# Gathering the first expert's rows before the last two attention steps, and adding theirs by one-hot products

## The chip, the core and the metric

The kernel runs on one core of one Trainium2 chip. The time is device microseconds of one launch, as the median of several runs. The core has five engines that run side by side, each with its own instruction queue: TensorE (PE, matmuls, with its weight loads shown as PEld), VectorE (DVE), ScalarE (ACT), GpSimd (POOL) and SyncE (SP, which here issues DMAs only). ACT and POOL issue DMAs too; the ones with an index list ("indirect") are POOL's. An engine works through its queue in order, so an instruction that waits holds up all that stand behind it.

## The reference, cut to what is computed

Two blocks follow one another. The first is a recurrent attention cell over 4 batches, 8 heads, 768 steps and a head size of 40. The second takes its output as 3072 rows of 320 numbers, sends every row to one of 8 experts by a hash of its token id, and runs that expert's two layers.

```python
for t in range(S):                                   # S = 768, state C and n per batch and head
    m_new = np.maximum(f_gate[:, :, t] + m, i_gate[:, :, t])
    f_stab = np.exp(f_gate[:, :, t] + m - m_new)
    i_stab = np.exp(i_gate[:, :, t] - m_new)
    C = f_stab * C + i_stab * outer(v[t], k[t])
    n = f_stab * n + i_stab * k[t]
    y[:, :, t] = sigmoid(o_gate[t]) * (C @ q[t]) / max(abs(n . q[t]), 1)
x = y.transpose(0, 2, 1, 3).reshape(3072, 320)
expert_idx = token_ids * 2654435761 % 8
for e in range(8):
    mask = expert_idx == e
    out[mask] = np.maximum(x[mask] @ w1[e], 0) @ w2[e]   # w1: 320 x 1024, w2: 1024 x 320
```

## The kernel before

**Attention.** Each batch is cut into 6 chunks of 128 steps, so there are 24 loop steps `s` (batch `b = s // 6`, chunk `c = s % 6`). Within a chunk the recurrence is a masked product with decay weights; between chunks a small state `C` is carried. A loop step writes its instructions in a fixed order, by hand (`tc.manual_schedule()`): loads, `decayed`, the turns of keys and queries (`turn_k`, `turn_q`), the turn back and finish of rows of an earlier step (`back`, `finish`), `decays` and `state` and `entering` for the chunks ahead, the stores of the finished rows (SP's queue), `scores` and `weigh` of the next chunk (`weigh` is L379 on DVE), routing work hung on the step (the lists `before` and `after`), and last `attend`, the products of the step itself (L422 with the carried state, L429 with the weights) and their copy out of PSUM (`hT` or `hB`, L445). In steps 5, 11, 15 and 18, which also carry a sigmoid of an output gate on ACT, that copy and two others are DVE's.

**Turn back and finish.** `back` turns a block of heads x time into time x heads with four transposes (L454). `finish` forms the denominator (L460, L463), multiplies by the gate (L466), takes the reciprocal (L469) and multiplies (L471, on POOL, for the very last block on DVE), and its result `x` is stored to the DRAM tensor `x_rows` (L477). Rows of batch `b - 1` are finished during batch `b`, one block of 128 for each step. For the last batch each block is finished one step after its attention, so steps 19 to 23 finish two blocks and one is left after the loop. PSUM tiles of the turns, decays and finishes share four buffers (the tag "tr").

**Routing.** Beside the loop the kernel counts the rows of each expert and gives every row a slot: each expert has 3 x 128 main slots and 32 remainder slots (416 in all, `CAP`); the remainders of four experts share one block of 128. Steps 12 to 19 turn slots into one-hot tables (`route_hot`), whose products of steps 13 to 20 (`route_table`) give the table of the row for each slot. After step 20 `route_index` makes the gather indices `g_idx` and the scatter indices `s_idx` of it on DVE (L643 to L647).

**Experts.** `fetch` gathers an expert's rows from `x_rows` with indirect DMAs on POOL (L842): three blocks of 128 and, for experts 0 and 4, the shared remainder block `xr`. `turns` transposes each block on PE (L865, L868), with DVE first copying the last 64 of the 320 columns a second time (L867), since that half block is used from both halves of the partitions, and DVE or ACT copying the result to `xT` (L870, L872). Expert 0's first layer is `layer1`, with products over 416 columns (L884, L891); the others use `layer1_pairs`, a form with fewer products, on sums of weight blocks and sums of row blocks (`sums_of_w1` on POOL, L936; `sums_of_x` on DVE, L942 to L946). The second layer is `layer2_pair` for all, with sums of `w2` on POOL (L1028), products L1044 and L1054, and DVE ops on their results (L1071 to L1082). Rows are scattered to the output by indirect DMAs on POOL (L852). Turns, sums and weight loads of later experts are called at set places between products (`between`).

At the start of this part stands an order that the change touches:

```python
fetch(0)
fetch(1)
later = weight_slices(1) + weight_slices(2)
...
spin(11)
for piece in turns(0):
    piece()
    spin(1)
```

`spin` runs products (L1138) whose result nobody reads, into a PSUM bank of their own. The weights in `later` are issued from ACT's queue, three slices at a `between`; those of experts 3 and on are issued from SP's queue.

The gate steps at the kernel's start (`gates_a`, `gates_b`, `gates_x`) use tiles `f_sb`, `i_sb`, `m_sb`, `fP` and so on, which lie in a pool that ends with the attention part.

Of the kernel before, what the change touches and what calls it, by code (L numbers as in the profile page):

```python
# [8 lines left out]
F32 = mybir.dt.float32  # L9
# [13 lines left out]
def kernel(  # L23
# [55 lines left out]

    x_d = nc.dram_tensor("x_rows", (N, Dm), F32, kind="Internal").ap()  # L80

    ident = consts.tile([P, P], F32, name="ident")
    g_idx = consts.tile([P, NC], I32, name="g_idx")
    s_idx = consts.tile([P, NC], I32, name="s_idx")
    xe = consts.tile([1, NX + 1], I32, name="xe")

    def weights(src1, src2, wpool, w2pool):
# [29 lines left out]
    with tc.tile_pool(name="gates", bufs=1) as gp, \  # L117
# [19 lines left out]
        Rs = [gp.tile([P, 2, H, P], BF16, name=f"R{i}") for i in range(2)]  # L137
        f_sb = gp.tile([BH, S], F32, name="f_sb")
        i_sb = gp.tile([BH, S], F32, name="i_sb")
        m_sb = gp.tile([BH, S + 1], F32, name="m_sb")  # L140

        at = [0, 2 * BH, 3 * BH]
        fP, iP, aP, AP, r1, r3 = (
            gp.tile([P, W2], F32, name=name) for name in ("fP", "iP", "aP", "AP", "r1", "r3")
        )
        mP = gp.tile([P, W2 + 1], F32, name="mP")
        keep = gp.tile([P, W2], F32, name="keep")
        zA = gp.tile([P, 6, W2], BF16, name="zA")
# [261 lines left out]
        def attend(s):  # L410
# [25 lines left out]
            b = s // NB  # L436
            if b == LB:
                hT[b, c] = wk.tile([P, 2, 2, P], F32, name="hT")[:]
                to = hT[b, c]
            else:  # L440
                if c == 0:
                    hB[b] = wk.tile([P, 2, 2, S], F32, name="hB")
                hT[b, c] = hB[b][:, :, :, c::NB]
                to = hB[b][:, :, :, c * P : (c + 1) * P]
            from_psum(s)(to, d["ht"][:, :, : 2 * P].rearrange("p f (i t) -> p f i t", t=P))  # L445
# [11 lines left out]
        def finish(b, r, xo):  # L457
            hs = xo.rearrange("p f i (x d) -> p f (i x) d", d=DP)
            den = wk.tile([P, 2, PR, 1], F32, name="den")
            nc.vector.tensor_scalar(  # L460
                den[:], hs[:, :, :, D:D1], scalar1=-1.0, scalar2=1.0, op0=ALU.mult, op1=ALU.max,
            )
            nc.vector.tensor_tensor(den[:], den[:], hs[:, :, :, D:D1], op=ALU.max)  # L463
            x = wk.tile([P, H, D], F32, name="x")
            xv = x.rearrange("p (j f) d -> p f j d", f=2)
            nc.vector.tensor_tensor(  # L466
                xv, hs[:, :, :, :D], gate(b, r).rearrange("p (j f) d -> p f j d", f=2), op=ALU.mult,
            )
            nc.vector.reciprocal(den[:], den[:])  # L469
            eng = nc.vector if (b, r) == (LB, NB - 1) else nc.gpsimd  # L470
            eng.tensor_tensor(xv, xv, den[:].to_broadcast([P, 2, PR, D]), op=ALU.mult)  # L471
            rows = x_d[b * S : (b + 1) * S, :]
            if b == LB:
                rows = rows[r * P : (r + 1) * P, :]
            else:
                rows = rows.rearrange("(p r) d -> p r d", r=NB)[:, r, :]
            return lambda: nc.sync.dma_start(rows, x.rearrange("p h d -> p (h d)"))  # L477

# [161 lines left out]
        def route_index():  # L640

            ta = gp.tile([P, NC], F32, name="ta")
            nc.vector.tensor_scalar(ta[:], tv[:], scalar1=-1.0, scalar2=0.0, op0=ALU.add, op1=ALU.max)  # L643
            nc.vector.tensor_copy(g_idx[:], ta[:])
            nc.vector.tensor_scalar(ta[:], tv[:], scalar1=0.0, scalar2=float(2 * N), op0=ALU.is_equal, op1=ALU.mult)
            nc.vector.scalar_tensor_tensor(ta[:], in0=tv[:], scalar=-1.0, in1=ta[:], op0=ALU.add, op1=ALU.add)
            nc.vector.tensor_copy(s_idx[:], ta[:])  # L647

        def second_l():
            nc.vector.tensor_copy(Ls[1][:HB], one[:HB, 0].to_broadcast([HB, S]))  # L650
            nc.sync.dma_start(Ls[1][HB:], Ls[0][HB:])


# [6 lines left out]
        after = {4: [route_counts], **{13 + i: [lambda i=i: route_table(i)] for i in range(NT // TH)}}  # L660
        after[12 + NT // TH].append(route_index)
        one = gp.tile([P, 2, 1], F32, name="one")
        turns_of = {c: (c,) for c in range(NB)}
# [96 lines left out]
        weigh(0)  # L760
        nc.sync.dma_start(tok[:], moe_token_ids.rearrange("(p t) -> p t", t=NT))
        slices = []

        o_loads = {3: [(0, 0)], 4: [(0, 1)], 6: [(1, 0)], 7: [(1, 1)], 8: [(2, 0)], 9: [(2, 1)]}
        o_loads.update({2 * NB + c: [(LB, c)] for c in range(NB)})
        for s in range(NT):
# [22 lines left out]
            if b + 1 < B:  # L789
                for r in (turns_of if b else first_turns).get(c, ()):  # L790
                    turn_q(b + 1, r, slice(r, None, NB), s)
            done = [(b - 1, c)] if b > 0 else []
            if b == LB and c > 0:
                done.append((b, c - 1))
            stores = [finish(*br, back(*br)) for br in done]
# [36 lines left out]
            for do in after.get(s, []):  # L832
                do()
        finish(LB, NB - 1, back(LB, NB - 1))()

# [94 lines left out]
    def sums_of_w1(w1t):  # L930

        a = [[w1t[:, k, :].rearrange("p (a i f) -> p i a f", i=2, f=P)[:, i] for k in range(2)] for i in range(2)]
        s1, s2, s3, s4 = s = [xp.tile([P, FB // 2, P], F32, name=f"ws{i}") for i in range(1, 5)]
        ops = ((s1, a[1][0], a[1][1], ALU.add), (s2, s1[:], a[0][0], ALU.subtract),
# [154 lines left out]
    with tc.manual_schedule():  # L1089
        xgs, xTs, remT, hrem = {}, {}, {}, {}  # L1090

# [9 lines left out]
        def turns(e):  # L1101
# [5 lines left out]
            def remainder():  # L1107
                i = e % EG
                if i == 0:
                    remT[e // EG] = xp.tile([P, DB, P], F32, name="remT")  # L1110
                    tp = turn(xgs[-1 - e // EG], remT[e // EG][:], True, e > 1)
                if e == 0:
                    nc.vector.tensor_copy(xT[:, :, NM:], tp[:, :, :RM])
                    return
                nc.scalar.copy(xT[:, :, NM:], remT[e // EG][:, :, i * RM : (i + 1) * RM])
# [12 lines left out]

        fetch(0)
        fetch(1)  # L1130

        later = weight_slices(1) + weight_slices(2)

        idle = mps.tile([P, CAP], F32, name="mh", tag="bank")

        def spin(n):
            for _ in range(n):
                nc.tensor.matmul(idle[:], lhsT=ident[:], rhs=W[0][0][:, 0, :CAP], start=True, stop=True)  # L1138

        spin(11)  # L1140
        for piece in turns(0):
            piece()
            spin(1)
        wsums, pieces, xss = None, [], {}
        for e in range(E):
# [3 lines left out]
            sums = sums_of_w2(W[e][2])  # L1149
            h = xp.tile([P, FB, CAP], F32, name="h")  # L1150
            if i == 0:
                hrem[g] = xp.tile([P, EG, FB, RM], F32, name="hrem")
            ahead = turns(e + 1) if e + 1 < E else []

            def one(_):
                if ahead:
                    ahead.pop(0)()
# [4 lines left out]
            def after(j):  # L1162
                if j == 0 and e + 1 < E:
                    xss[e + 1] = sums_of_x(xTs[e + 1])
# [27 lines left out]
    with tc.If(nx > 0):  # L1192
        with tc.For_i(0, nx, 1) as k:
# [11 lines left out]
            xT = xp.tile([P, DB, CAP], F32, name="xT")  # L1205
            h = xp.tile([P, FB, CAP], F32, name="h")
            gather(xr[:, :Dm], gs[:, 0:1])
# [33 lines left out]
```

## Time and profile before

| | |
|---|---|
| median of 3 runs | 406.95 us (406.87 to 408.23) |
| profiled execution: time, span | 408.27 us, 406.5 us |
| mean granted TensorE clock | 0.98 |
| PE busy | 382.9 us (94%) |
| PEld busy | 313.8 us (77%) |
| DVE busy | 219.9 us (54%) |
| ACT busy | 146.6 us (36%) |
| POOL busy | 201.5 us (50%) |
| idle products, L1138 | 30 passes between 160.0 and 172.2 us |

The span is that of the instructions in the profiled execution; the time beside it is that execution's own, and the median is that of other runs. Busy times are sums over stages with different limits: attention lasts until about 160 us, the experts from there on. A product of f32 numbers shows as two passes in the trace.

### The profile page before, as it was taken

What the parts mean: (1) busy time and instruction counts of PE and PEld (TensorE: products, weight loads), DVE (VectorE), ACT (ScalarE), POOL (GpSimd) and SP (SyncE); (2) the same over time, 40 slices, a digit from 0 to 9 for tenths busy, and PEclk for the clock granted to TensorE, in tenths of its full rate; (3) what the DMA queues carried; (4) which work ended last, traced back from release to release, by engine and by line L of the source; (5) the groups of instructions that cost most, each with busy time, mean ns of one, the idle gap of its engine ahead of it and who ended that gap; (6) DMA issues with size and microseconds to landing.
All of it is one profiled execution on the core that took longest, in us unless ns stands there. A gap on an engine that the chain in (4) does not pass through costs nothing. (4 is left out here: it accounts for less than half of the span.)

```text
span 406.5 us, 8793 instructions
## 1 busy us (share of the span) xinstructions
PE 382.9 (94%) x3406; PEld 313.8 (77%) x3406; DVE 219.9 (54%) x526; ACT 146.6 (36%) x281; POOL 201.5 (50%) x253
## 2 busy tenths in 40 slices
PE   8689979999999998999999999999999999999991
PEld 7567868777877775556998988977989889889771
DVE  7656657768796874235246347354345463452500
ACT  6334785577566541011113232141231141321300
POOL 6653103323434641784297495682592883907011
PEclk9959999999999999999999999999999999999996
DMA  7587756978777512357968136244235201000000
GB/s 143 106 197 158 198 107 158 243 186 165 150 155 182 142 55 81 98 167 222 332 218 263 61 110 214 82 121 141 91 125 164 81 2 47 2 15 34 0 17 35
DMA packets 96165, 51.46 MB, mean 127 GB/s; under 512 B 68022, under 2 KB 90170, under 8 KB 96122
## 3 DMA queue, kind: packets, MB, share of 16 engines
q1 hardware_dynamic: 88330, 36.65, 36.1%
q0 software_dynamic: 2496, 8.20, 6.4%
q10 hardware_dynamic: 5296, 6.03, 4.6%
q8 instruction: 28, 0.46, 0.5%
q14 instruction: 15, 0.12, 0.1%
HBM read 41.98 MB, written 8.63 MB: 125 GB/s over the span
## 5 line engine op out<-in xcount | busy, mean ns | idle before, releaser
L852 POOL DMA_INDIRECT out_dram<-zo,s_idx x26 | 26.9, 1035 | 88.7 <-DVE zo L1082 52.1
L471 POOL TENSOR_TENSOR x<-x,den 128x320 f32<-128x320 f32 x23 | 16.6, 723 | 52.1 <-DVE den L469 27.1
L379 DVE TENSOR_TENSOR w<-sp,w 128x512 f32<-128x512 f32 x48 | 30.9, 686 | 13.6 <-PE sp L371 13.0
L1044 PE MATMUL zp<-w2t,h 128*128 128x320 f32 x128 | 36.5, 438 | 0.0
L1044 PEld LDWEIGHTS zp<-w2t,h 128*128 128x128 f32 x128 | 23.3, 190 | 11.4 <-issue 2.1
L371 PE MATMUL sp<-qT,kT 64*128 64x128 f32 x384 | 29.4, 291 | 2.4 <-ACT qT L308 1.6
L371 PEld LDWEIGHTS sp<-qT,kT 64*128 64x128 f32 x384 | 24.6, 193 | 9.1 <-issue 4.4
L1014 ACT ACTIVATE h<-h 128x832 f32<-128x832 f32 x14 | 12.6, 898 | 47.6 <-DVE h L1013 47.6
L334 ACT ACTIVATE w<-ab 128x512 f32<-128x512 f32 x48 | 26.6, 608 | 8.3 <-PE ab L330 8.3
L842 POOL DMA_INDIRECT xg<-x_rows,g_idx x24 | 23.3, 973 | 12.4 <-issue 12.4
L1054 PE MATMUL zp<-t,s 128*128 128x160 f32 x192 | 27.7, 300 | 0.6 <-DVE s L1039 0.6
L1054 PEld LDWEIGHTS zp<-t,s 128*128 128x128 f32 x192 | 26.5, 190 | 1.1 <-POOL ws L936 0.8
L429 PE MATMUL ht<-w,v 128*64 128x128 f32 x384 | 27.1, 285 | 0.0
L1028 POOL TENSOR_TENSOR t<-w2t,t 128x640 f32<-128x640 f32 x16 | 24.7, 1544 | 0.6
L962 PE MATMUL mb<-xs,ws 128*128 128x208 f32 x112 | 25.0, 346 | 0.0
L1028 POOL TENSOR_TENSOR t<-w2t 128x640 f32<-128x640 f32 x16 | 24.8, 1553 | 0.1
L962 PE MATMUL ma<-xT,w1t 128*128 128x208 f32 x112 | 24.8, 346 | 0.0
L429 PEld LDWEIGHTS ht<-w,v 128*64 128x64 f32 x384 | 21.2, 140 | 4.0 <-issue 3.1
L330 PE MATMUL ab<-R,L 128*64 128x512 bf16 x96 | 16.3, 400 | 5.0 <-DMA R<-R 2.6
L962 PEld LDWEIGHTS mb<-xs,ws 128*128 128x128 f32 x112 | 19.6, 190 | 1.8 <-issue 1.8
L962 PEld LDWEIGHTS ma<-xT,w1t 128*128 128x128 f32 x112 | 18.9, 190 | 1.8 <-issue 1.8
L1054 PE MATMUL zp<-w2t,h 128*128 128x160 f32 x128 | 20.2, 301 | 0.0
(252 smaller groups left out, 876.9 us busy)
## 6 DMA issues: line engine op xcount, KB each, us to landing
w2t<-in_moe_w_dram SPq DMA_DIRECT2D x24, 320.0 KB
w1t<-in_moe_w_dram SPq DMA_DIRECT2D x24, 256.0 KB
k<-in_k_dram SPq DMA_DIRECT2D x24, 160.0 KB
v<-in_v_dram SPq DMA_DIRECT2D x24, 160.0 KB
x_rows<-x SPq DMA_DIRECT2D x24, 160.0 KB
ql<-in_q_dram SPq DMA_DIRECT2D x6, 480.0 KB
og<-in_o_gate_dram SPq DMA_DIRECT2D x6, 480.0 KB
w2t<-in_moe_w_dram ACTq DMA_DIRECT2D x8, 320.0 KB
```

Of the source, the lines that this page charges most:

```text
L330: nc.tensor.matmul(ab[i * HB : (i + 1) * HB], lhsT=Ls[b % 2][:, c * P + i * HB : c * P + (i + 1) * HB], rhs=R[:, i, hf::2, :], start=True, ...
L334: nc.scalar.activation(w[:, hf], ab[:], AF.Exp)
L371: nc.tensor.matmul(sp[hf][:, j, :], lhsT=d["kT"][r, j, :], rhs=q_of(s)[r, j, :], start=True, stop=True,)
L379: nc.vector.tensor_tensor(d["w"][:, hf], d["sp"][hf][:], d["w"][:, hf], op=ALU.mult)
L429: nc.tensor.matmul(place(j, hf), lhsT=d["v"][:, 2 * j + hf, :], rhs=d["w"][:, hf, j, :], start=(c == 0 and j0 == 0), stop=True, skip_group ...
L471: eng.tensor_tensor(xv, xv, den[:].to_broadcast([P, 2, PR, D]), op=ALU.mult)
L842: nc.gpsimd.indirect_dma_start(out=xg, out_offset=None, in_=x_d[:, :], in_offset=bass.IndirectOffsetOnAxis(ap=idx, axis=0),)
L852: ins = nc.gpsimd.indirect_dma_start(out=out[:, :], out_offset=bass.IndirectOffsetOnAxis(ap=idx, axis=0), in_=zo[:], in_offset=None, bound ...
L962: nc.tensor.matmul(dst[:, i, :], lhsT=x(2 * q + i), rhs=y, start=(start and i == 0), stop=stop, skip_group_check=True,)
L1028: nc.gpsimd.tensor_tensor(d[:], x, y[:] if y in (t1, t2) else y, op=ALU.subtract)
L1044: nc.tensor.matmul(zp[:], lhsT=h[:, fb, 2 * P : 3 * P], rhs=w2t[:, fb, :], start=(fb == 0), stop=(fb == FB - 1),)
L1054: nc.tensor.matmul(dst, lhsT=x[:, i], rhs=y[:, i], start=(start and i == 0), stop=(i == FB // 2 - 1), skip_group_check=True,)
```

## The change

- `x_rows` gets one more row, at index `NL = 3072 - 256`, filled with zeros. The rows of the last two loop steps (22 and 23, called late) lie behind it.
- Expert 0's rows are gathered by a list of their own, `g_first`, in which every late row is replaced by the row of zeros. The four gathers are issued by POOL in loop step 23, ahead of that step's finish.
- The slots of all rows are written to DRAM and those of the 256 late rows are read back, one per partition (`lslot`). In steps 15 to 22 DVE builds a table of 0 and 1 (`ones0`) from them, 128 late rows by 512 slots for each of the two late blocks.
- The late blocks are kept in SBUF (`xl`) as they are finished, both by DVE alone. Products of `xl` with `ones0` give the late rows at their slots, already transposed: three products for each late block, 512 columns wide. They are added by DVE to the transposed gathered rows.
- Rows of batch 2 are finished one step earlier, two in step 18 and none in step 23. The last batch's attention results go to one tile (`hB`), as those of the other batches do.
- The idle products at the start of the experts are gone. Expert 1's first turn is at the second place instead of the first, and its `sums_of_x` one place later in expert 0's second layer.
- The new tiles take 4960 words of each partition for the whole kernel (`both`). The gate steps' tiles lie in the same memory. The tiles `h` and `ws` have one buffer instead of two.

Cut to its core (line numbers in the text are those of the kernel before; L643 to L647 are `route_index`):

```diff
+    NL = N - 2 * P
+    x_d = nc.dram_tensor("x_rows", (N + 1, Dm), F32, kind="Internal").ap()
+    slots_d = nc.dram_tensor("slots", (N,), F32, kind="Internal").ap()
...
+    g_first = consts.tile([P, NJ + 1], I32, name="g_first")
+    both = consts.tile([P, 4960], F32, name="both")
+    xg0 = both[:, :1536].rearrange("p (j d) -> p j d", d=DB * P)
+    xl = both[:, 1536:2304].rearrange("p (k d) -> p k d", d=DB * P)
+    ones0 = both[:, 2304:3328].rearrange("p (k c) -> p k c", c=4 * P)
+    xT0 = both[:, 3328:4576].rearrange("p (d c) -> p d c", c=CAP)
+    remT0 = both[:, 4576:4960].rearrange("p (d c) -> p d c", c=P)
...
+        f_sb, i_sb, m_sb = both[:BH, 2308:3076], both[:BH, 3076:3844], both[:BH, 3844:4613]
+        fP, iP, aP, AP, r1, r3 = (both[:, i * W2 : (i + 1) * W2] for i in range(6))
+        mP, keep = both[:, 2048 : 2049 + W2], both[:, 4616 : 4616 + W2]
...
+            late = b == LB and r >= NB - 2
+            x = xl[:, r - NB + 2, :Dm] if late else wk.tile([P, Dm], F32, name="x")
...
-            eng = nc.vector if (b, r) == (LB, NB - 1) else nc.gpsimd
+            eng = nc.vector if late else nc.gpsimd
             eng.tensor_tensor(xv, xv, den[:].to_broadcast([P, 2, PR, D]), op=ALU.mult)
...
+            if late:
+                nc.scalar.copy(xl[:, r - NB + 2, Dm:], x[:, 2 * P :])
+                row0 = b * S + r * P + 1
+                rows = x_d[row0 : row0 + P, :]
...
             nc.vector.tensor_scalar(ta[:], tv[:], scalar1=-1.0, scalar2=0.0, op0=ALU.add, op1=ALU.max)
+            gm = gp.tile([P, NJ + 1], F32, name="gm")
+            for lo, n, c in ((0, NJ, 0), (NJ, 1, NR)):
+                nc.vector.tensor_scalar_min(gm[:, lo : lo + n], ta[:, c : c + n], float(NL))
+            nc.vector.tensor_copy(g_first[:], gm[:])
+            nc.vector.scalar_tensor_tensor(ta[:], in0=ta[:], scalar=float(NL), in1=ta[:], op0=ALU.is_ge, op1=ALU.add)
             nc.vector.tensor_copy(g_idx[:], ta[:])
...
+        def route_last(k, j):
+            c0 = NR * P if j == NJ else j * P
+            nc.vector.tensor_scalar(
+                ones0[:, k, j * P : (j + 1) * P], iota_f[:], scalar1=float(c0), scalar2=lslot[:, k : k + 1],
+                op0=ALU.add, op1=ALU.is_equal,
+            )
...
+        before[11].append(lambda: nc.sync.dma_start(slots_d.rearrange("(p t) -> p t", t=NT), sl[:]))
+        before[13].append(lambda: nc.sync.dma_start(lslot[:], slots_d[NL:].rearrange("(k p) -> p k", p=P)))
+        for i in range(8):
+            before.setdefault(15 + i, []).append(lambda i=i: route_last(i // 4, i % 4))
...
         nc.sync.dma_start(tok[:], moe_token_ids.rearrange("(p t) -> p t", t=NT))
+        zrow = gp.tile([1, Dm], F32, name="zrow")
+        nc.gpsimd.memset(zrow[:], 0.0)
+        nc.sync.dma_start(x_d[NL : NL + 1, :], zrow[:])
...
-            done = [(b - 1, c)] if b > 0 else []
-            if b == LB and c > 0:
-                done.append((b, c - 1))
+            done = [(b - 1, c)] if 0 < b < LB else []
+            if b == LB:
+                done = [(b - 1, r) for r in ((0, 1) if c == 0 else (c + 1,)) if r < NB]
+                if c > 0:
+                    done.append((b, c - 1))
+            if s == NT - 1:
+                for j in range(NJ + 1):
+                    nc.gpsimd.indirect_dma_start(
+                        out=xg0[:, j, :Dm], out_offset=None, in_=x_d[: NL + 1, :],
+                        in_offset=bass.IndirectOffsetOnAxis(ap=g_first[:, j : j + 1], axis=0),
+                    )
...
-        finish(LB, NB - 1, back(LB, NB - 1))()
+        om = [ps.tile([P, PR, P], F32, name=f"sp{i}").rearrange("p j t -> p (j t)") for i in range(2)]
+        om.append(ps.tile([P, 2, 512], F32, name="ht")[:, 0, :])
+        def rows_by_table(k, db):
+            nc.tensor.matmul(
+                om[db], lhsT=xl[:, k, db * P : (db + 1) * P], rhs=ones0[:, k, :], start=(k == 0), stop=(k == 1),
+                skip_group_check=True,
+            )
+        rows_by_table(0, 0)
+        xo = back(LB, NB - 1)
+        rows_by_table(0, 1)
+        rows_by_table(0, 2)
+        finish(LB, NB - 1, xo)()
+        for j in range(NJ + 1):
+            tp = ps.tile([P, DB, P], F32, name="tp0", tag="tr", bufs=4)
+            for db in range(2):
+                nc.tensor.transpose(tp[:, db, :], xg0[:, j, db * P : (db + 1) * P], ident[:])
+            nc.scalar.copy(xg0[:, j, Dm:], xg0[:, j, 2 * P : Dm])
+            nc.tensor.transpose(tp[:, 2, :], xg0[:, j, 2 * P :], ident[:])
+            if j < NJ:
+                nc.scalar.copy(xT0[:, :, j * P : (j + 1) * P], tp[:])
+            else:
+                nc.scalar.copy(remT0, tp[:])
+                nc.scalar.copy(xT0[:, :, NM:], tp[:, :, :RM])
+        for db in range(DB):
+            rows_by_table(1, db)
+        for db in range(DB):
+            nc.vector.tensor_tensor(xT0[:, db, :], xT0[:, db, :], om[db][:, :CAP], op=ALU.add)
+            nc.vector.tensor_tensor(remT0[:, db, :], remT0[:, db, :], om[db][:, NM:], op=ALU.add)
...
-        fetch(0)
         fetch(1)
...
-        spin(11)
-        for piece in turns(0):
-            piece()
-            spin(1)
...
-                if ahead:
+                if ahead and (e > 0 or fp != 0 or len(ahead) < 4):
                     ahead.pop(0)()
...
-                if j == 0 and e + 1 < E:
+                if j == (e == 0) and e + 1 < E:
                     xss[e + 1] = sums_of_x(xTs[e + 1])
```

## The prediction

> **What bounds the kernel now.** First, on the page, the forty slices: TensorE (PE) is busy almost everywhere, at a full granted clock but for one slice near the start and the end.
>
> ```profile
> PE   8689979999999998999999999999999999999991
> ...
> PEclk9959999999999999999999999999999999999996
> ```
>
> Busy need not mean useful, so next the timeline around the hand-over from attention to experts (start, busy time, engine, line, tiles, count, idle time before and its releaser).
>
> ```profile
> 156.56 1.09 PE L429 MATMUL ht<-w,v 128*64 128x128 f32 x16
> ...
> 160.08 0.49 DVE L471 TENSOR_TENSOR x<-x,den 128x320 f32<-128x320 f32 x1
> 160.08 7.92 PE L1138 MATMUL mh<-w1t,ident 128*128 128x416 f32 x22 [1.02 <-DVE den L469]
> ...
> 163.37 1.19 POOL L842 DMA_INDIRECT xg<-x_rows,g_idx  x1 [5.41 <-issue]
> ...
> 166.71 0.38 DVE L867 COPY xg<-xg 128x64 f32<-128x64 f32 x1 [6.14 <-DMA xg<-x_rows,g_idx]
> ...
> 172.67 3.06 PE L891 MATMUL mh<-xT,w1t 128*128 128x416 f32 x8 [0.46 <-issue]
> ```
>
> The last attention product ends at 157.65, the first expert's first product starts at 172.67: 15.02 us of latencies, which PE fills with the idle products of L1138. They are: turn back and finish (x at 160.57), 2.80 until the first gather starts, 3.34 from there to its first user, then four gathers about 1.25 apart and the turns. After 172.67 PE is dense to 397.8 (the list of waits gives the PE engine one of 0.6 us), so whatever moves 172.67 moves the end.
>
> Then the loop step 21, where VectorE (DVE) makes the index tables, and expert 0's second layer:
>
> ```profile
> 144.44 0.19 DVE L644 CAST g_idx<-ta 128x47 int32<-128x47 f32 x1
> ...
> 146.94 0.68 DVE L346 TENSOR_TENSOR qs<-qT,xb 128x512 f32<-128x512 f32 x1
> ...
> 147.62 0.67 PE L422 MATMUL ht<-qs,C 64*64 64x128 f32 x16
> ```
>
> ```profile
> 197.61 0.33 DVE L1074 TENSOR_TENSOR u<-zp,u 128x160 f32<-128x160 f32 x1 [0.69 <-PE zp L1054]
> ...
> 198.49 1.27 PE L1054 MATMUL zp<-t,h 128*128 128x160 f32 x8
> ```
>
> In step 21 PE starts L422 at 147.62, just as DVE ends qs: DVE sets the pace. In the second layer PE needs L1074, and has 0.55 us to spare. Last, the clock by windows (PE busy, then the other engines; the number after five engines is the granted clock):
>
> ```profile
> 17.95:21.36 3.41, 0.96 (x20) 0.93 (x21) 3.34 (x8) 1.88 (x4) 2.82 (x5) 1.00 0.82 143
> 21.36:24.77 3.41, 2.56 (x21) 1.94 (x17) 2.90 (x7) 1.08 (x4) 2.37 (x9) 0.50 0.90 206
> ```
>
> After 3.41 us with PE busy for 0.96, the clock fell to half at 21.36; it came back at 31.6.
>
> **The junction, from the last attention product's end (0) to the first expert's first product.** The four gathers now follow the stores of step 22. There x was finished at 152.63; by the 2.80 above they start at 155.4, and by their old spacing and 3.34 they land at 158.7, 160.2, 161.4 and 162.7: 1.1 to 5.1 on this scale. What is late next is the chain of the last rows:
> - First table product: 512 columns in two passes. L1138 starts a 416-column pass every 0.35, so 0.43 a pass and 0.86 a product: 0.86.
> - Turn back, 0.66: 1.52. Finish on DVE, 1.51 (159.06 to 160.57): 3.03. ScalarE (ACT) pads, 0.24 and a hand-over: 3.30. PE meanwhile does the other two first products (1.72), until 3.24.
> - Four turns go through ACT alone: pad 0.24, hand-over 0.05, third transpose 0.32, hand-over 0.15, copy 0.47 (L870): 1.23 each, 4.92: 8.22. The extra 32-column copy, 0.26: 8.48. PE ends the last transpose at 7.60.
> - Three second products: 8.46, 9.32, 10.18.
> - DVE adds, 0.59 each for 416 columns (L992 has that shape) and 0.22 for 128 (between the small ops of 0.19 and the 0.28 of L408): the third pair ends at 11.06. In the built order the first expert's first product carries the only DVE wait, and the later ones of the block none, so I count all adds: 11.1.
>
> 15.0 - 11.1 = 3.9 us saved. The gathers have 2 us to spare at each turn (their pads are wanted at 3.3, 4.5, 5.8 and 7.0). Three w1 loads of 256 KB now stand earlier on ACT's queue, issued at about 0.8 to 2.1, beside the last gathers; no row shows a gather under such load, so 0 to 2 us, and I take 0 for that slack. The idle products go: no work is lost; the clock's risk is among the rivals.
>
> **What the loop pays.**
> - Step 18 gets one more turn back (batch 2 now runs one row ahead), step 23 one fewer. In step 18 PE runs without a gap, and a second turn back in step 21 cost about 0.6: +0.6. Step 23's PE waits for ACT's hT until 155.38 anyway: 0 back.
> - Four small DVE ops before g_idx, spaced 0.22 as L643 to L647 are, in the step that DVE paces: +0.85. Behind them queue finish, C, qs and weigh.
> - Eight one-hot ops of 128x128, about 0.2 (a third of the 0.55 of the 128x384 L624). Behind six of them DVE waits 0.5 to 1.1 for PE before its next L460 or L637; those of steps 15 and 18 stand ahead of DVE's own PSUM copies (L445) in stretches without a gap: 2 x 0.2 = +0.4, between 0 and 1.6.
> - The zero row's store stands on SyncE's (SP) queue and waits for GpSimd's (POOL) memset behind L233, which ends at 22.44. Behind it queue v, half of ql, the input pieces, k and q; they were issued from 20.58 on, so are 2.4 us later. They are for steps 2 and 3 or later; DMA share there is about 1. Moved traffic can help or hurt the R loads for which PE waits near 30: -0.5 to +1.0, taken as 0.
> - Slots stored and read back, two small SP issues of about 0.4 two steps apart, then two steps until use: 0.
> - First-rows buffers in the gates' memory: the built order gives the gate steps the same waiters, so 0. One buffer for h: its old readers are before its new writers on PE, 0. One for ws: GpSimd writes ws for expert 7 at 349.65, expert 6's last read ends at 350.40; 0.75 us on POOL, with over 10 us until PE wants it: 0.
>
> Sum +1.85, from 0.3 to 3.5.
>
> **Expert 0.** sums_of_x now comes after L1071 (ends 196.92) and ahead of L1074. Its five ops span 1.86 us, so L1074 goes from 197.61 to about 198.8, and PE's product from 198.49 to 199.15: +0.66. Gathers for expert 1 start at the last store plus 2.8, before its turns, and GpSimd's w2 sums end earlier than they did: 0.
>
> **Sum.** -3.9 + 1.85 + 0.66 = -1.4 us. The profiled execution took 408.27 with a span of 406.5; it is 1.3 above the median of 406.95, a difference inside the runs' own spread. A change of a stage applies to either, so 406.95 - 1.4 = 405.55.
>
> **Rivals.**
> *The loop hides what is added.* If PE's gaps take the step-18 and DVE ops as they take the other steps', -3.9 + 0.3 + 0.66 = -2.9, at most -4.4 with a gain at the start: 402.5 to 404. For: DVE's waits for PE, up to 1.08 before an L460. Against: the 147.62 above.
> *The clock falls at the junction (slower).* Without idle products PE does three transposes (0.5 busy) per 1.23 us for 4.3 us: 41% of a window. The window with 28% fell, the one from 157.89 with 1.89 of 3.42 (55%) did not; the point that decides is between them, and whether a window falls inside the stretch. Half clock for 10.24 us, as from 21.36 to 31.6, less 1.5 of PE idle, costs 4.4: -1.4 + 4.4 = +3.0, 409.9. If it lasts one window of 3.41 with 0.9 of idle, 1.3: -0.1. The trace shows 10.24, so I price it by that, with 1.3 as the bound.
> [...]
> *The change does not do what it says:* the gathers wait for the last stores after all. Then the old 13 us until the last gather lands stay, the products and adds come on top (about 3): 409 to 411. Against: in the built order the first gather waits for two stores, those of step 22.
>
> **Numbers.** A measurement of this kernel tells about 0.5% from no change: 404.9 and 409.0. Forecast 0.52, of which a third lies below 404.9; hidden loop 0.22, nearly all faster; clock 0.21, a half of it same; gathers late 0.05. Faster 0.36, same 0.46, slower 0.18. The forecast alone spans 404.0 to 407.2; with the hidden loop below and the clock above, 402.8 to 409.3.
>
> **What would show it.** Right: first gather about 2.3 us before the last attention product ends; first L962 about 11 us after it (15 before); four ACT copies 1.2 us apart; the last attention product 1 to 2.5 us later than 157.65; a gap of 0.7 in expert 0's second layer. Wrong: a granted clock below 1.00 between the junction and expert 0's end; a first gather that follows the last store; the loop's end at 157.65 or beyond 160.7; new PE gaps from expert 1 on.

## The result, and the profile after

The changed kernel takes 407.74 us (median of 4 runs, 407.3 to 408.41) beside 407.25 for the kernel before: ratio 1.001, 95% interval 0.9986 to 1.0033. Run again later (run 10) it gave 408.65 beside 407.9, ratio 1.002 (0.9997 to 1.0043). So the measurement cannot tell it from no change; the medians lie 0.5 and 0.75 us above before's, where the forecast, 405.55, lay 1.4 below the 406.95 that it started from.

The profiled execution took 408.41 with a span of 406.7, against 408.27 and 406.5. The slices of the page, PE busy and granted clock, now have a dip where attention hands over to the experts, PE at slices 16 and 17 and the clock at slice 17:

```profile
PE   8779979999999997899899999999999999999991
...
PEclk9969999999999999699999999999999999999997
```

The timeline of that hand-over in the changed kernel (start, busy, engine, line, tiles, count, idle time before and its releaser):

```profile
155.07 1.19 POOL L831 DMA_INDIRECT both<-x_rows,g_first  x1 [3.43 <-DMA x_rows<-x]
...
155.46 1.09 PE L438 MATMUL ht<-w,v 128*64 128x128 f32 x16
...
161.55 0.44 PE L893 MATMUL tp<-ident,both 128*128 128x128 f32 x2 [1.15 <-DMA both<-x_rows,g_first]
...
163.56 0.69 PE L893 MATMUL tp<-ident,both 128*128 128x128 f32 x2 [1.41 <-DMA both<-x_rows,g_first]
...
165.44 3.62 PE L880 MATMUL sp<-both 128*128 128x512 f32 x4
168.86 1.28 PE L880 MATMUL ht<-both 128*128 128x512 f32 x2
171.10 1.28 PE L962 MATMUL mh<-both,w1t 128*128 128x416 f32 x3 [0.97 <-DVE both L905]
```

The gathers start where the prediction put them, 1.5 us before the last attention product ends at 156.55 (it had said 2.3). But the second and third are not used before 161.55 and 163.56, 5.0 and 5.7 us after their starts at 156.56 and 157.82 (3.34 in the kernel before), and PE stands still for 2.6 us. Then four passes of L880 take 3.62 us; at a full clock two products were to take 1.72. The windows between clock changes say why (PE busy first; behind the five engines the granted clock, DMA share, GB/s):

```profile
159.13:162.54 3.41, 1.80 (x8) 0.76 (x6) 0.46 (x1) 1.46 (x5) 0.89 (x1) 1.00 0.97 334
162.54:165.95 3.41, 2.34 (x7) 1.40 (x8) 0.00 (x0) 1.27 (x5) 0.58 (x1) 0.50 0.18 71
165.95:169.36 3.41, 3.41 (x5) 1.35 (x4) 1.04 (x3) 0.35 (x2) 2.50 (x4) 0.50 0.33 96
```

In the first window the DMA share is 0.97 (334 GB/s): that is where the three early w1 loads run, issued from 156.92 on. PE is busy for only 1.80 of 3.41 us, and the clock falls for two windows, until 169.36. The other places that the prediction had shown, step 21 and expert 0's second layer, look like this:

```profile
144.00 0.19 DVE L659 CAST g_idx<-ta 128x47 int32<-128x47 f32 x1
...
146.50 0.68 DVE L355 TENSOR_TENSOR qs<-qT,xb 128x512 f32<-128x512 f32 x1
...
146.63 0.67 PE L431 MATMUL ht<-qs,C 64*64 64x128 f32 x16
```

```profile
194.20 2.44 PE L1125 MATMUL zp<-t,s 128*128 128x160 f32 x16 [0.41 <-ACT p L1139]
...
198.50 1.32 PE L1125 MATMUL zp<-t,h 128*128 128x160 f32 x8 [0.77 <-DVE zo L1146]
```

L431 starts while DVE still writes qs: the two don't belong together. And the second layer now waits twice, for ACT's copy into the tile p and for DVE's result zo. Both traces cut at the same events add up to the 0.2 us between the spans (score products are those issued in the step named; s is another tile of the second layer, whose wait stands in both kernels):

| stretch | before | changed | difference |
|---|---|---|---|
| start to the score products of step 1 | 32.19 | 31.06 | -1.13 |
| step 1 to step 15 | 79.79 | 78.66 | -1.13 |
| step 15 to step 22 | 39.88 | 41.09 | +1.21 |
| to the end of the last attention product | 5.79 | 5.74 | -0.05 |
| to the first expert product | 15.02 | 14.55 | -0.47 |
| to the end of PE's wait of 0.64 us for s | 75.83 | 77.46 | +1.63 |
| to the end | 157.96 | 158.12 | +0.16 |

### The profile page after: what moved, and what is told of

Same layout as the page of the kernel before. It is cut to its first block, busy times and chain, and to the rows that moved or that the text cites. A ratio compares the mean times of both kernels' runs of the same rounds, so it can differ in the third digit from the quotient of the medians.

```text
span 406.7 us, 8792 instructions
## 1 busy us (share of the span) xinstructions
PE 380.3 (94%) x3388; PEld 311.2 (77%) x3388; DVE 222.6 (55%) x538; ACT 148.8 (37%) x290; POOL 200.7 (49%) x253
## 5 line engine op out<-in xcount | busy, mean ns | idle before, releaser
L1115 PEld LDWEIGHTS zp<-w2t,h 128*128 128x128 f32 x128 | 23.3, 190 | 11.1 <-issue 1.8
L913 POOL DMA_INDIRECT xg<-x_rows,g_idx x21 | 20.2, 962 | 11.4 <-issue 5.8
L450 ACT COPY hB<-ht 128x512 f32<-128x512 f32 x20 | 11.7, 587 | 29.6 <-PE ht L438 27.0
L1007 POOL TENSOR_TENSOR ws<-w1t 128x512 f32<-128x512 f32 x14 | 18.3, 1309 | 3.9 <-DMA w1t<-in_moe_w_dram 3.1
```

Source lines behind the costliest of these rows:

```text
L913: nc.gpsimd.indirect_dma_start(out=xg, out_offset=None, in_=x_d[:, :], in_offset=bass.IndirectOffsetOnAxis(ap=idx, axis=0),)
L1007: return s, [lambda o=o: nc.gpsimd.tensor_tensor(o[0][:], o[1], o[2], op=o[3]) for o in ops]
L1115: nc.tensor.matmul(zp[:], lhsT=h[:, fb, 2 * P : 3 * P], rhs=w2t[:, fb, :], start=(fb == 0), stop=(fb == FB - 1),)
```

## The experiments

Line numbers shift by a few between kernels; "stretch" is the time from the end of the last attention product to the first expert product.

**1. The early weight loads, later (e1).** From the changed kernel:

```
-                for _ in range(3):
+                for _ in range(0 if e == 0 and fp == 0 and len(later) == 20 else 3):
```

> The first three weight loads of expert 1 are issued behind the first expert's turns instead of ahead of them. Theory A (the early weight loads slow the gathers, the transposes starve, and the poor windows let the TensorE clock fall for 6.8 us): gathers 2 and 3, used 4.97 and 5.7 us after their start in the changed kernel, are ready some 3.4 us after it, the two waits of 1.15 and 1.41 us for them go, and the time from the end of the last attention product to the first expert product falls from 14.55 us to about 12 (11 if the clock then stays at 1.00); time 404.5 to 405.5 us. Rival B (the gathers are late by themselves, or the clock falls anyway because the turns alone leave PE poor): the clock still falls, the stretch stays over 13.5 us, time 407 to 408. Rival C (whatever the junction saves is lost to later weights for expert 1): stretch about 11 to 12, but a new wait for a weight in expert 1, time about 407.

406.26 us beside 407.19, ratio 0.9977 (0.9959 to 0.9994), above the 404.5 to 405.5 expected. PE waits for no gather any more; the four turns start 1.04 us apart. The stretch is 12.20 us. The clock still falls, once and later:

```profile
161.63:165.04 3.41, 1.92 (x11) 1.08 (x10) 0.00 (x0) 2.15 (x7) 0.74 (x1) 1.00 0.32 96
165.04:168.45 3.41, 3.41 (x6) 1.14 (x4) 1.57 (x4) 0.30 (x2) 2.50 (x4) 0.50 0.33 96
```

So the loads made the gathers late, as A says; and B is right that the turns by themselves leave PE poor enough (1.92 of 3.41) for the clock to fall.

**2. Idle products behind the turns (e2).** From the changed kernel, with the early loads kept:

```
+        def fill(n):
+            for _ in range(n):
+                nc.tensor.matmul(htl[:, 1, :416], lhsT=ident[:], rhs=W[0][0][:, 0, :416], start=True, stop=True)
...
             nc.tensor.transpose(tp[:, 2, :], xg0[:, j, 2 * P :], ident[:])
+            fill(1)
```

> One product of the identity with a weight tile, 416 columns, whose result nobody reads, follows each of the four turns; the early weight loads stay. Theory A: the gathers stay as late as they were (PE waits of 1 to 1.5 us for gathers 2 and 3), but the windows of 3.41 us no longer fall under the share at which the clock drops: clock 1.00 throughout, the second table products 0.86 us each instead of 1.28, the stretch from attention to the first expert product 14.55 us less 2 to 3, time 405 to 406. Rival B (the clock follows something else, or the waits are too long for one product each): the clock still falls and the stretch keeps its 14 to 15 us, time 407.5 to 408.5.

The clock holds: the two windows of the turns have PE busy for 2.80 and 2.73 us of 3.41. The gathers stay late, as both their lines show:

```profile
161.70 0.44 PE L899 MATMUL tp<-ident,both 128*128 128x128 f32 x2 [0.57 <-DMA both<-x_rows,g_first]
...
163.69 0.44 PE L899 MATMUL tp<-ident,both 128*128 128x128 f32 x2 [0.68 <-DMA both<-x_rows,g_first]
```

The stretch is 12.97 us, 1.6 below the changed kernel's, less than the 2 to 3 expected; the time does not show it: 407.43, ratio 1.0001 (0.9983 to 1.002). In the profiled execution PE waits 1.05 us for p in expert 0 (runs 4, 7 and 8 take that up), where the changed kernel's waited 0.41.

**3. Both edits (e3).** Those of runs 1 and 2, on the changed kernel.

> The edits of the two runs ahead together: weight loads later, one idle product behind each turn. Theory A: gathers in time and clock 1.00: stretch about 11 us (the sum of the prediction, 11.1, plus what the four products of some 0.7 us put on the path, 0 to 1), time 404 to 405. Rival B: the junction is not bound by either, stretch over 13 us, time 407 to 408.

405.09 us, ratio 0.9956 (0.9937 to 0.9975). The stretch is 11.21 us, the clock stays at 1.00, and the last of the table's adds ends 11.06 after the last attention product. The prediction's chain has 11.06 too, but by two differences that cancel (below). Neither edit alone does this. The line that ends it:

```profile
167.94 1.29 PE L969 MATMUL mh<-both,w1t 128*128 128x416 f32 x3 [0.97 <-DVE both L912]
```

**4. The kernel before without its idle products (e4).** The other side of the clock's account, from before:

```
-        spin(11)
         for piece in turns(0):
             piece()
-            spin(1)
```

> The kernel before without its twelve-fold idle product and without the one behind each turn. Theory A (a stretch of waiting and turning without idle products loses the clock): the clock falls by half for 6.8 to 10.2 us at the junction, and the time rises by 3 to 5 us, to 410 to 412. Rival B (the clock holds, since the turns' own work is enough, or the stretch is bound by gathers and ACT so that a slower TensorE costs nothing): 407 to 408.

409.09 us, ratio 1.0052 (1.0026 to 1.0077): +1.9, under the 3 to 5 expected. The clock fell behind an empty window and came back four windows later:

```profile
157.37:160.78 3.41, 0.00 (x0) 0.00 (x0) 0.85 (x3) 0.00 (x0) 0.00 (x0) 1.00 0.14 48
...
164.19:167.60 3.41, 2.82 (x9) 1.44 (x9) 1.20 (x4) 0.48 (x1) 2.50 (x4) 0.50 0.53 141
167.60:171.01 3.41, 1.86 (x6) 1.06 (x6) 1.12 (x4) 0.48 (x1) 2.79 (x3) 0.50 0.48 141
171.01:174.42 3.41, 3.41 (x7) 1.63 (x6) 0.00 (x0) 0.00 (x0) 2.80 (x3) 0.50 0.96 342
```

Most of the half clock falls on waiting, so it costs less than its length: the first eight expert passes take 5.18 us instead of 3.06. The idle products of before were worth their place. This run, too, has PE waiting for p (1.16 us), with expert 0 in the old order.

**5. One more store on SyncE's queue (e5).** To before, at the zero row's place (z_d is a scratch row in DRAM):

```
+        nc.sync.dma_start(z_d[:, :], ident[:1, :])
```

> The kernel before with one more store of a row on SyncE's queue, 512 bytes of the identity into a scratch row, at the place of the zero row; nothing else. In every run of the changed kernel's family the o_gate load of step 8 leaves SyncE's queue after 0.76 to 0.96 us instead of 1.49 to 1.72, PE's wait of 0.35 to 0.50 us for R is gone, and step 11 is 0.36 us shorter: the distance from the score products of step 1 to those of step 15 is 78.66 to 78.69 us instead of 79.79. Theory A (the added store moves every later load of the queue by one place, and that is all that shortens the steps): the distance is 78.7 here too, time 1.1 us below the kernel before, 406.1. Rival B (something else of the change does it, such as other addresses of the tiles): the distance stays at 79.6 to 79.8, time 407.2.

Step 1 to 15 takes 79.01 us. The two profiles with the loop of before (before itself and run 4) have 79.79 and 79.62, nine profiles with the changed loop 78.66 to 78.91 (the tenth, run 8, runs past step 1 at half clock and is left out). Step 11 is 6.06 us as in the changed kernel, where before and run 4 have 6.42 and 6.41; step 8 is 5.80, between the 6.07 and 6.21 of those two and the 5.49 of the changed kernel. The line behind step 8, in the kernel before and then here:

```profile
75.55 1.72 SPq L179 DMA_DIRECT2D og<-in_o_gate_dram  x1
```

```profile
73.53 0.90 SPq L180 DMA_DIRECT2D og<-in_o_gate_dram  x1
```

So the added store alone brings most of those 1.1 us. The time, 406.83, ratio 0.9989 (0.9965 to 1.0013), is too rough to say so. How one store more shortens a later load's issue is open, and the issue's length alone does not set step 8: in run 6 it is 1.18 us and the step 5.49.

**6. Expert 0 in the old order (e6).** To run 3:

```
-                if ahead and (e > 0 or fp != 0 or len(ahead) < 4):
+                if ahead:
                     ahead.pop(0)()
...
-                if j == (e == 0) and e + 1 < E:
+                if j == 0 and e + 1 < E:
```

> The run with both edits (weight loads later, one idle product behind each turn), and expert 0 as in the kernel before: the first turn of expert 1 at the first place, and the sums of its rows behind the first product of layer 2. Theory A (the moved turn and sums cost expert 0 its stalls): the waits of 0.41 to 1.05 us for p and of 0.77 us for zo are gone, the stretch from the first expert product to the 0.64 us wait for s goes from 76.83 us back to the 75.8 of the kernel before, time 404.0. Rival B (expert 1's rows are not there in time): PE waits for the rows at the first place, 0.5 to 2 us, and the clock may fall again, time 405 to 407.

406.96 us, ratio 0.9988 (0.9957 to 1.0019). The wait for zo is gone; waits of 0.34 us for p and 0.24 for s stand in the second layer, so the order is not what makes p late. The stretch is 12.23 us, 1.0 longer than in run 3. On DVE:

```profile
166.50 0.40 DVE L945 COPY xg<-xg 128x64 f32<-128x64 f32 x1 [5.91 <-DMA xg<-x_rows,g_idx]
166.60 0.58 DVE L911 TENSOR_TENSOR both<-both,sp 128x416 f32<-128x416 f32 x1
```

With the turn at the first place, the copy of expert 1's rows stands on DVE ahead of the table's adds, and waits for its gather. B is right that far, and it is what the change avoids by moving the turn; but the last pair of adds starts only 0.2 us later behind its product than in run 3. The other 0.8 us is ACT's last copy of hB, which starts 1.1 us after the product that it waits for (0.1 in run 3), and PE waits for that copy. ACT's instructions up to there are those of run 3; run 7, on the same chip, shows the same (1.4 us), no other profile does; why the copy starts late is open. The time settles nothing here.

**7. One-hot operations of steps 15 and 18 moved (e7).** To run 6:

```
-            before.setdefault(15 + i, []).append(lambda i=i: route_last(i // 4, i % 4))
+            before.setdefault((16, 16, 17, 17, 19, 20, 21, 22)[i], []).append(lambda i=i: route_last(i // 4, i % 4))
```

> The run ahead, with the one-hot operations of steps 15 and 18 put into steps 16 and 17 beside those that stand there. Theory A (the 0.44 us operation lies on the path in steps 15 and 18 alone, where it stands ahead of the eviction of the state products on DVE): the steps 15 to 16 and 18 to 19 become 0.35 us shorter each (6.75 to 6.40, 6.20 to 5.85), and steps 16 and 17, where PE had no wait for DVE, stay; time 0.7 below the run ahead, 403.3. Rival B (two operations in a step come on the path there): 0 to 0.5 above that.

Step 15 to 16 takes 6.40 us and step 18 to 19 5.85, to the hundredth what was expected, and no other step grew. So these two operations cost 0.7. The time, 405.96, ratio 0.9989 (0.9959 to 1.0019), does not stand out, as PE's wait for p is 1.63 us in the profiled execution. ACT at that place:

```profile
190.45 2.02 ACTq L114 DMA_DIRECT2D w1t<-in_moe_w_dram  x2
192.52 0.29 ACT L1146 COPY p<-zp 128x160 f32<-128x160 f32 x1 [3.00 <-DMA w2t<-in_moe_w_dram]
```

The copy of p comes behind weight loads on ACT's queue, whose issue waits for an earlier load.

**8. No loads ahead of p (e8).** To run 3 with the moved one-hot operations:

```
-                for _ in range(0 if e == 0 and fp == 0 and len(later) == 20 else 3):
+                for _ in range(0 if e == 0 and fp in (0, "after 0") else 3):
```

> The run with both edits (weight loads later, one idle product behind each turn; expert 0 as the change has it), with the one-hot operations of steps 15 and 18 in steps 16 and 17, and with no weight loads issued behind the first product of layer 2 of expert 0. Theory A (p is copied by ACT late because ACT's queue holds three weight loads ahead of the copy, which wait for an earlier load): PE's wait for p, which was 0 to 1.63 us from run to run, in kernels of both families, is gone; the wait of 0.77 us for zo stays; steps 15 to 16 and 18 to 19 take 6.40 and 5.85 us; from the first expert product to the wait for s 76.6 to 76.9 us; time 404.3 to 404.6. Rival B (p waits for something else): its wait stays between 0.3 and 1.6 us, time 405 or more.

"after 0" names the place behind the first product of the second layer. 404.46 us beside 407.9, ratio 0.9924 (0.9897 to 0.995). The wait for p is gone; ACT copies it as soon as PE has it, ahead of the loads:

```profile
191.68 0.29 ACT L1146 COPY p<-zp 128x160 f32<-128x160 f32 x1 [0.49 <-PE zp L1132]
192.80 0.38 ACTq L114 DMA_DIRECT2D w2t<-in_moe_w_dram  x1
```

First expert product to the wait for s is 76.56 us, 0.73 above before's 75.83: the zo wait.

**9. Two turns at the second place (e9).** To run 8:

```
+                    if e == 0 and fp == 1:
+                        ahead.pop(0)()
...
-                if j == (e == 0) and e + 1 < E:
+                if j == 0 and e + 1 < E:
```

> The run ahead with two turns of expert 1 at the second place of expert 0 (none at the first, as the change has it), so that the sums of its rows can stand behind the first product of layer 2 again. Theory A (the wait of 0.77 us for zo is DVE, busy with the sums that the change put one place later; the kernel where the turn was put back to the first place held the table's adds behind a copy of expert 1's rows, which waited for a gather until 166.5 us): wait for zo gone, the adds start with their product as in the changed kernel (first expert product 11.2 us after the last attention product), first expert product to the wait for s 75.8 to 76.1 us; time 0.7 below the run ahead, 403.6 to 403.9. Rival B (the second turn at that place finds its rows not there): a wait of 0.3 to 1.5 us for them, time as the run ahead or above.

405.23 us, ratio 0.9951 (0.9924 to 0.9978): not better than run 8. The zo wait is gone, and its size comes back as the second turn's wait for its rows' copy on DVE, as B has it:

```profile
176.88 0.33 PE L946 MATMUL tp<-ident,xg 128*128 128x128 f32 x1 [0.94 <-DVE xg L945]
```

**10. The changed kernel again.**

> The changed kernel as it is, again, on the same chip as the two runs ahead, so that the last of them can be compared with it. Theory A: 407.5, within 0.3% of the kernel before, the clock half for 6.8 us at the junction. If the first result was a matter of few runs: 405.5 or less.

408.65, told above. The loads delay the gathers as in the first profile (waits of 0.80, 1.43 and 0.29 us), but the clock is half for one window, 165.55 to 168.97, not two: the windows lie elsewhere in this execution. The stretch is 13.56 us.

**11. Three idle products instead of four (e10).** To run 8, whose fourth lies behind the last turn:

```
-            fill(1)
+            if j < NJ:
+                fill(1)
```

> The kernel with the later weight loads, moved one-hot operations and ACT's copy ahead of its loads, with the idle product left out behind the fourth turn alone: in the run with both edits the second table products begin 7.50 us after the last attention product, behind four idle products; in the run without any they begin at 6.80. Theory A (the first three lie beside ACT's copies, the fourth is on the path): second products at 6.8, first expert product 10.5 us after the last attention product, clock 1.00, time 0.7 below 404.5, 403.8. Rival B (the clock falls again without the fourth, or the last copy of ACT holds the adds): 11.2 or more, 404.5 to 406.

403.43 us beside 407.81, ratio 0.9899 (0.9857 to 0.9942). Second table products 6.79 and first expert product 10.50 us after the last attention product (156.23), the clock at 1.00:

```profile
163.02 1.88 PE L886 MATMUL sp<-both 128*128 128x512 f32 x4
164.74 1.02 PE L886 MATMUL ht<-both 128*128 128x512 f32 x2
166.73 0.94 PE L970 MATMUL mh<-both,w1t 128*128 128x416 f32 x2 [0.97 <-DVE both L913]
```

This version beats both kernels: about 1.0% below the kernel before.

## Why the prediction was right or wrong

The forecast, 405.55, did not come true: 407.74 lies above the 407.2 to which the forecast alone reached, and inside the whole range only because the rival of the falling clock was counted in. That the time ends so near to no change is luck. In the two traces the junction gave 0.5 us instead of 3.9 and expert 0 cost 1.0 more than forecast, while a loop that cost 1.8 less, and a start that was 1.1 shorter in this execution, gave 2.9 back.

**The chain of the junction was right, its cover wrong.** Freed of loads and clock (run 3) the chain has nearly the predicted length, 11.21 for 11.1, but that the two agree so well is luck. One term was mis-sized, the turns: 1.04 us each, not 1.23, which is 0.8 less for the four; and the idle product behind the fourth, which the sum does not have, puts 0.7 back. Without it the stretch is 10.50 (run 10). (The third pair of adds, by the sum's own figures, ends at 10.18 + 0.59 + 0.22 = 10.99, not 11.06.) Two things that I set at nothing took the gain in the changed kernel:
- *The early w1 loads* ("0 to 2 us, and I take 0 for that slack"). They cost PE 2.6 us of waiting for gathers, which came 1.6 to 2.4 late. The slack of 2 us a turn was not there either: by the 3.34 the second gather would have been usable at 159.90, and PE was ready for it at 160.40 (161.55 less its wait), so the slack was 0.5. The gathers began 1.5 us before the last attention product's end and not 2.3, and the shorter turns want them earlier. The end that I took was the one no row spoke for.
- *The clock.* This was the second rival, which I gave 0.21, and it is what happened: the clock fell for two windows (6.8 us, between the 10.24 and the one window that I had priced; runs 1 and 10 do show one of 3.41 there), where the kernel before had held it with its idle products. Moving the loads alone takes the stretch from 14.55 to 12.20 us, holding the clock alone to 12.97, both to 11.21; so the two gains, 2.35 and 1.58, overlap by 0.6, since PE also waits while its clock is half (1.02 of the 1.41 us ahead of 163.56 lie behind the fall at 162.54). The 12.97 and the 11.21 still hold the 0.7 of the fourth idle product; without it the clock's part would be about 2.3. The deciding point was put between 28% and 55% of a window. The runs show no single one: the clock fell behind windows with 49%, 53% and 56% (1.68 us in run 10, 1.80 in the changed kernel, 1.92 in run 1), and held behind others with 50%, 52%, 55% and 56% (near the start 1.70 in run 5, 1.79 in run 7 and 1.91 in run 3; 1.89 in before, at 157.89) and with 80% (2.73, run 2). The windows differ in what PE does as well: of the three that lost the clock 1.3 to 1.6 us are transposes, of the four that held it at 50 to 56% 0 to 0.8 us. No run separates the two. The 41% that I had for the turns was 56% in run 1, and the clock fell.

**The loop's sum of +1.85 came out as +0.08 from step 1 to step 22, by errors of both signs.** Step 18's extra turn back: +0.6 predicted, +0.55 measured (5.42 to 5.97). One-hot operations: +0.4 predicted, 0.7 shown by run 7; the two steps were the right ones, the operations took 0.44 us there and not 0.2. The four index operations: +0.85 predicted, 0 measured (that step is 5.84 us in both). That step failed in its reading of the trace: I took two times that meet, the end of qs and PE's L422, for a wait, though no wait stood on that line. By the code, entering(s + 1) makes the qs of the next step, so nobody on PE was waiting for the 0.6 us that DVE lost (from L647 to the next L465 2.06 us; from L637 to L460 1.48 before). The zero row, taken at 0 with a gain of up to 0.5: the trace was 1.13 shorter from step 1 to 15, and run 5 gives most of that to a store on that queue.

**The start is in part the clock's and in part the change's.** The -1.13 ahead of step 1 goes with the length of the half clock there, which differs from execution to execution, as does the place of its fall: it lasted 10.2 us in the profile of before, and in run 1 (falls at 21.36 and 21.70), and both reach step 1 at 32.19; 6.8 us in the changed kernel and runs 2, 3, 6, 9, 10 and 11 (falls at 21.03 in run 9, at 22.02 to 22.91 in the others), which reach it at 31.01 to 31.43. The half clocks here and at the junction last 3.41 us (here in runs 5 and 7, there in runs 1 and 10), 6.83, 10.24 or 13.65 (here in run 8, there in run 4), so one to four times 3.413: that is the window of this text. But where the clock falls and returns at nearly the same times, the changed loop is later than the loop of before. Run 9 reaches step 1 at 31.29 and run 4 at 30.06 (clock back at 27.86 and 27.63); run 7 at 31.30 and run 5 at 30.18 (27.30 and 27.24). In runs 9 and 7 PE waits there for a load into L (1.05 and 1.29 us), in runs 4 and 5 no such wait shows; run 5, then run 7:

```profile
28.96 0.62 PE L331 MATMUL ab<-R,L 128*64 128x512 bf16 x4
```

```profile
30.09 0.62 PE L339 MATMUL ab<-R,L 128*64 128x512 bf16 x4 [1.29 <-DMA L<-input_pieces]
```

In run 7 the zero row's store leaves SyncE's queue at 23.06, behind the memset that ends at 23.03, and what stands behind it leaves 3 us later than in run 5, whose added store waits for no memset. The DMA share is 0.10 from 22 to 24 us and 1.10 from 26 to 28, where that load is on its way; in run 5 it is 1.03 and 0.28. So the zero row, taken at 0 with a loss of at most 1.0, cost about 1.1 to 1.2 us in these two pairs. No run takes its wait alone away, so that part is argued. With the 10.2 us of half clock no such difference shows.

**Expert 0: +0.66 predicted, +1.63 measured.** The zo wait is the step I had, 0.77; run 9 removes it by undoing the order of the sums. I had not looked at ACT's queue: p came 0.41 us late behind the weight loads, which run 8 removes; that is not the change's alone, since before shows it too when its timing shifts (run 4). The remaining 0.45 is smaller waits that I can't put to one cause; in run 8 they are gone.

**The other rivals.** The gathers did not wait for the last stores; the first one's releaser is a store of step 22. The loop did not hide what was added: steps 15 to 22 paid 1.21, and the gain of 1.13 ahead of them, which the rival did not have, offset it. (The rival's "at most -4.4" does not follow from the bounds given: -2.9 with 0.5 gained at the start is -3.4.)

## What to carry to other kernels

Where a chain of short waits replaces idle products, count PE's busy share in stretches of 3.41 us first: here windows with PE busy for 49 to 56% lost the clock in some places and held it in others, and three products that nobody reads, put beside copies that take longer anyway, cost nothing (second table products at 6.79 us in run 11, at 6.80 without any in run 1) and kept the clock at 1.00. Issue bulk loads behind the small latency-bound transfers of a junction, and behind the copies on the same engine's queue that another engine waits for; the one cost 2.6 us of waiting here, the other up to 1.6. Two times in a trace that meet are not a wait: check in the code that the one reads what the other writes.

## What was not expected of the hardware

- The first gather of 128 rows was usable 3.34 us after its start in the kernel before (DMA share 0.27 in that time); in the changed kernel the second and third were after 5.0 and 5.7, with a window of share 0.97 (334 GB/s) in that time.
- Windows in which PE was busy for half the time were enough for the clock to fall (1.68 to 1.92 of 3.41 us, runs 10 and 1 and the changed kernel). At half clock, windows with PE busy for 2.34 (changed kernel) and 2.82 of 3.41 us (run 4) did not bring it back; in each of these a window with 3.41 did. In the changed kernel the two falls, at 22.58 and 162.53, are 139.95 us apart, 41 times 3.413.
- In run 8 the half clock near the start lasted four windows, 21.77 to 35.42, although PE shows as busy for the whole of the second (3.42 us). A full window did not bring the clock back in the kernel before (24.77 to 28.19) and in run 1 (25.11 to 28.53) either, so one is not always enough; in those two the clock came back behind the next window, with 2.83 and 3.18. Why is open.
